# Turning q and k over two slots, x^T in halves, and the last four weight conversions moved behind the first batch

## The chip, the cores and the metric

The kernel runs on one core of a Trainium2 chip. The metric is device time in microseconds, the median of several executions.

## The reference

Attention with a threshold, for 8 batches of 8 heads, 576 rows and head size 64, then a two-layer MLP with exact GELU over the 4608 rows of 512:

```python
scores = scale * np.matmul(q, k.transpose(0, 1, 3, 2))
thresh = np.max(scores, axis=-1, keepdims=True) - tau
scores = np.where(scores >= thresh, scores, -1000000000.0)
attn = np.exp(scores - np.max(scores, axis=-1, keepdims=True))
attn = attn / (np.sum(attn, axis=-1, keepdims=True) + 1e-09)
attn_out = np.matmul(attn, v)
x = attn_out.transpose(0, 2, 1, 3).reshape(B * S, H * D)
h = x @ w_in
out = (0.5 * h * (1.0 + erf(h / sqrt(2)))) @ w_out
```

q, k, v are float32. The MLP's weights (512x2048 and 2048x512) arrive as 64-bit floats, so the kernel has to turn them into float32 itself.

## The kernel before

**Slots.** Two heads make a pair; a pair p has five chunks of query rows (four of 128 rows for each head, the fifth with the 64 left of both). One (pair, chunk) is a slot n, and the order of the work is a list written out by hand (lines 1103 to 1107): slots 0 to 7 take chunks 0 and 1 of the four pairs of batch 0, slots 8 to 19 their chunks 2 to 4, and from slot 20 (`BATCH`) on each pair goes through its five chunks in turn, pairs 4 to 31. All instructions of a slot are issued in the order of the loop body at line 1137, and each engine keeps to that order.

**What a slot does.** `scores` (L400) multiplies on TensorE into one or two PSUM tiles "sc", of which there are two buffers. `softmax_head` takes the row maximum on VectorE (L412), the threshold on GpSimd (L415) and the exponential on ScalarE (L417). `softmax_tail` masks and sums on VectorE (L433), and so frees the "sc" buffers for the next slot's scores. In the first batch p is transposed on TensorE one slot later (`turn_p_early`, L347, with copies by ScalarE at L354 and L362); from pair 4 on VectorE transposes it (`turn_p`, L532) and DMAs regroup it. `weigh_v` (L571) multiplies with v to x^T; the early `weigh_half` (L603) does it for one chunk of 128 rows. All TensorE outputs other than scores share four PSUM buffers "mm"; each is free again when its copy has been made.

**Turning q and k.** In the first batch `turn_qk_early` transposes q and k of the next pair on TensorE (L317, and L327 for the tails of 64 rows); ScalarE copies them out (L320 and L322, tails L330 and L331, and the two q tails at L334). It is called once in the first slot of the pair before (line 1150), that is in slots 0, 2 and 4 for pairs 1, 2 and 3. Raw q and k of pair 2 lie in two slots of `xall`.

**x^T of the first batch.** A list `due` names what is multiplied with v in the next slot. Pairs 2 and 3 (`HALVED`) have x^T of their first 256 rows made in two halves, in slots 6 to 9; pairs 0 and 1 have it made whole, in slots 3 and 5. `divide_early` (L490, L492, L498) follows with the second half or the whole.

**Weights.** 32 pieces of 128x512 are loaded as raw 64-bit values, pieces 0 to 15 of w_in and 16 to 31 of w_out; even ones go to a slot of `xall` (seven slots, some of which hold x), odd ones to a part of `turned_p`, apart from the last `LATER`, which go to `xall` too. A conversion has three parts: two activations on ScalarE (`convert_first`, L199 and L200), two operations on VectorE (`convert_second`, L207 and L208), and one add on GpSimd (`add_low_bits`, L219). The add is issued in the next slot's `softmax_head`: that of the newest piece ahead of the first L415, the others behind the second. `STEPS` says how many conversions a slot ends with. The intermediate `power` comes from the pool "g" of 10 buffers, which also holds the hidden activations of an MLP block.

**The MLP in between.** `fill` issues the products of MLP blocks of 256 rows between the attention's work: the hidden layer at L671, the output layer at L686, up to a goal for each slot. A product is issued only when the number of pieces whose add has been issued is large enough: j of the output layer needs 17 + j. The hidden layer of block 0 lies in slots 10 to 19. In slot 20 its held GELUs run (L644), and in slot 21 the output layer begins. The last part of the kernel (from line 1260) runs ten blocks with a fast scheme on sums of tiles (L859, L741).

Of the kernel before, what the change touches and what calls it, by code (L numbers as in the profile page):

```python
# [9 lines left out]
U32 = mybir.dt.uint32  # L10
U8 = mybir.dt.uint8
AF = mybir.ActivationFunctionType
# [6 lines left out]
def kernel(  # L19
# [28 lines left out]
    nc = tc.nc  # L48
    ctx.enter_context(tc.manual_schedule())

    B, H, S, D = q.shape
    d_model, d_ff = moe_w_in.shape
    P = 128
    Q = 32
    HP = H // 2
    NP = B * HP
    EARLY = HP
    NC = S // P
    MAIN = NC * P
    TAIL = S - MAIN  # L60
# [5 lines left out]
    TOK = 256  # L66
# [32 lines left out]
    x_free = list(range(XSLOTS))  # L99
    x_at = {}  # L100

    def x_slot(want=None):
        i = max(x_free) if want is None else want
        x_free.remove(i)
        return i
# [8 lines left out]
    def x_rows(i):  # L114
        return xall[:, i, :, :].rearrange("p c t -> p (c t)")
# [5 lines left out]
    ident = const.tile([P, P], FP32, name="ident")  # L121
# [3 lines left out]
    q_tail = [att.tile([P, P], FP32, name=f"q_tail{i}") for i in range(4)]  # L125
# [3 lines left out]
    pd = [turned_p[:, e, :, :, :].rearrange("p h b i -> p (h b i)") for e in range(2)]  # L129
# [8 lines left out]
    q_scale = const.tile([P, 1], FP32, name="q_scale")  # L138
# [7 lines left out]
    for _ in range(3):  # L146
# [3 lines left out]
    PIECE = 512  # L150
    pieces = [(w_in_sb[c][:, f:f + PIECE], moe_w_in[c * P:(c + 1) * P, f:f + PIECE])
              for f in range(0, d_ff, PIECE) for c in range(N_DM)]
    pieces += [(w_out_sb[j][:, f:f + PIECE], moe_w_out[j * P:(j + 1) * P, f:f + PIECE])
               for j in range(N_DF) for f in range(0, d_model, PIECE)]
    wide = moe_w_in.dtype != FP32
    LATER = 2
    raws = []
    loaded = [0]
    converted = [0]

    def load_piece(eng=nc.sync):
        k = loaded[0]
        if k == len(pieces):
            return
        staged = k % 2 and k < len(pieces) - LATER
        if wide and not staged and not x_free:
            return
        dst, src = pieces[k]
        loaded[0] += 1
        if not wide:  # L170
            nc.sync.dma_start(dst, src)
            converted[0] += 1
            load_piece()
            return
        slot = []
        if staged:

            half, at = divmod(k // 2 % 4, 2)
            raw = pd[half].bitcast(U32)[:, at * 2 * PIECE:(at + 1) * 2 * PIECE]
        else:  # L180
            slot = [x_slot()]
            raw = x_rows(slot[0]).bitcast(U32)
        eng.dma_start(raw, src.bitcast(U32))
        raws.append((dst, raw, slot))

    ahead = []

    def convert_first():

        dst, raw, slot = raws.pop(0)
        lo, hi = (raw.rearrange("p (f w) -> p f w", w=2)[:, :, i] for i in range(2))
        power = gp.tile([P, PIECE], U32, tag="g", name="power")
        nc.scalar.activation(power.bitcast(FP32), hi.bitcast(FP32), AF.Copy, bias=0.0, scale=2.0 ** -112)  # L199
        nc.scalar.activation(dst.bitcast(U32), lo, AF.Copy, bias=0.0, scale=2.0 ** -29)  # L200
        ahead.append((dst, hi, power, slot))
# [20 lines left out]
    def convert_ahead(steps):  # L222

        while raws and len(ahead) <= steps:
            convert_first()

    def convert(steps):

        while steps > 0 and (ahead or raws):
            convert_ahead(1)  # L230
            convert_second()
            steps -= 1

# [62 lines left out]
            for c in range(2):  # L296
                nc.tensor.matmul(idle[:, c * P:(c + 1) * P], lhsT=ident, rhs=ident, start=True, stop=True)

    def turn_qk_early(p):


        s = st[p]
        if 2 <= p < HP:
            qT = op.tile([P, MAIN], FP32, tag="o_sb", name="qT")
            kT = pd_tail[p - 2].rearrange("p b i -> p (b i)")
        else:
            qT = ld.tile([P, MAIN], FP32, tag="qT", name="qT")
            kT = ld.tile([P, TAIL + S], FP32, tag="kT", name="kT")
        s["qT"], s["kT"] = qT, kT
        qt = s["q_tail"] = q_tail[p % 4]  # L310
        copy = nc.scalar.copy if p else nc.vector.tensor_copy
        for name in "qk":
            t = s[name]
            tr = ps.tile([P, NC, P], FP32, tag="mm", name="tr")
            for c in range(NC):
                for e in range(2):
                    nc.tensor.matmul(tr[e * D:(e + 1) * D, c, :], lhsT=t[:, e, c, :], rhs=ident, start=True, stop=True)  # L317
            src = tr.rearrange("p c s -> p (c s)")
            if name == "q":
                nc.scalar.activation(qT, src, AF.Copy, bias=0.0, scale=q_scale)  # L320
            else:
                copy(kT[:, TAIL:S], src)  # L322
        tr = ps.tile([P, NC, P], FP32, tag="mm", name="tr")
        for j, name in enumerate("qk"):
            t = s.pop(name)
            for e in range(2):
                nc.tensor.matmul(tr[e * D:(e + 1) * D, j, 0:TAIL], lhsT=t[0:TAIL, e, NC, :],  # L327
                                 rhs=ident[0:TAIL, 0:TAIL], start=True, stop=True)
        x_free.extend(s.pop(name + "_slot") for name in "qk" if name + "_slot" in s)
        nc.scalar.copy(kT[:, S:S + TAIL], tr[:, 1, 0:TAIL])  # L330
        nc.scalar.copy(kT[D:P, 0:TAIL], tr[D:P, 1, 0:TAIL])  # L331
        for e in range(2):
            rows = slice(e * D, (e + 1) * D)
            nc.scalar.activation(  # L334
                qt[rows, e * TAIL:(e + 1) * TAIL], tr[rows, 0, 0:TAIL], AF.Copy, bias=0.0, scale=q_scale[rows])

    def turn_p_early(p, i):

# [140 lines left out]
    def divide_early(p, lo, hi):  # L479


        s = st[p]
        b, hp = divmod(p, HP)
        tr = ps.tile([P, 512], FP32, tag="mm", name="tr")
        for i in range(lo // P, -(-hi // P)):
            den = s.pop(("sum", i))
            to = tr[:, i * P - lo:min((i + 1) * P, hi) - lo]
            for e in range(2):
                one_of, cols = (den[:, e:e + 1], ident) if i < NC else (den, ident[:, e * TAIL:(e + 1) * TAIL])
                nc.tensor.matmul(to[e * D:(e + 1) * D, :], lhsT=one_of.to_broadcast([P, D]), rhs=cols, start=True, stop=True)  # L490
        by = dg.tile([P, S], FP32, tag="inv", name="inv")
        nc.scalar.copy(by[:, 0:hi - lo], tr[:, 0:hi - lo])  # L492
        for n, o, at, size in in_blocks(b, lo, hi):
            x, y = x_blk[n][:, hp, o:o + size], by[:, at - lo:at - lo + size]
            if size == TOK:
                x = x.rearrange("q (p c) -> q c p", c=2)
                y = y.rearrange("q (c p) -> q c p", c=2)
            nc.gpsimd.tensor_tensor(x, x, y, op=ALU.mult)  # L498
# [595 lines left out]
    for _ in range(4):  # L1094
        load_piece(nc.sync)
# [12 lines left out]
    BATCH = HP * SLOTS  # L1108
# [15 lines left out]

    PARTS = 1.3, 1.3, 0.2, 1.3, 0.9

    HALVED = (2, 3)
    DIVIDE_LATE = {14: 0, 16: 1, 19: 2, 22: 3}
    STEPS = [0, 1, 1, 1, 1, 1, 2, 1, 2, 2, 2, 2, 3, 2, 2, 3, 2, 2, 2]
    BUSY = {1: 2, 6: 2, 8: 2}  # L1130

    tokens = 0
# [1 line left out]
    due = []  # L1134
    leaving = []
    loads = iter(())
    for n in range(len(slots) + WEIGH + 1):
        p, i = slots[n] if n < len(slots) else divmod(n, SLOTS)
        early = p < EARLY
        last = slots[n - 1] if 0 < n <= len(slots) else None  # L1140
        if p < NP:
            scores(p, i)
            softmax_head(p, i)
            add_low_bits()
            if last and last[0] < EARLY and last[1] < 2:
                invert(*last)
            if last and last[0] < EARLY and last[1] == NC:
                divisors_early(last[0])
            if p < HP - 1 and i == 0:
                turn_qk_early(p + 1)  # L1150
        elif n == len(slots):
            early_end.close()
            weights_first()
# [5 lines left out]
        for args in due:  # L1159
            if len(args) == 2:  # L1160
                weigh_half(*args)
                if args[1]:
                    divide_early(args[0], 0, TOK)
                continue
            if n == BATCH:
                xT = weigh_v(*args, None)
                continue
            weigh_v(*args)
            if args[1] == 0:
                divide_early(*args)  # L1170
        due = []
        if long:
            convert_ahead(STEPS[n] if n < BATCH - 1 else LATER)
        if n in DIVIDE_LATE:
            divide_late(DIVIDE_LATE[n])
        if p > EARLY and i == WEIGH:
# [51 lines left out]
            scale_q(p + 1)  # L1228
        if p >= HP - 1 and i == 2 and p + 1 < NP:
            turn_qk(p + 1)  # L1230
        convert(STEPS[n] if n < BATCH - 1 else len(pieces))
        if not early:
            lag[0] = 2 if p < NP else 0
            if n != BATCH:
# [3 lines left out]
        if n in BUSY:  # L1238
            keep_busy(BUSY[n])
        if last and last[0] < EARLY:  # L1240
            if last[1] < 2 and last[0] in HALVED:
                due.append((last[0], last[1]))
            elif last[1] == 1:
                due.append((last[0], 0, TOK))
            if last[1] == NC and early:
                due.append((last[0], TOK, S))
            if n == BATCH - 1:
                due.append((p, TOK, S))
# [44 lines left out]
```

## Time and profile before

| | |
|---|---|
| median of three executions | 1331.73 us (1331.51 to 1331.79) |
| the profiled execution, its own time | 1331.37 us |
| its span, first to last instruction | 1329.2 us |
| TensorE busy | 1315.9 us |
| VectorE busy | 1040.7 us |
| ScalarE busy | 604.3 us |
| GpSimd busy | 635.2 us |
| granted TensorE clock | 0.999 |

Cut at the first L412 of each slot, the slots that the change touches took:

| slot | window, us | length | PE busy | DVE busy | ACT busy | POOL busy |
|---|---|---|---|---|---|---|
| 2 | 18.65 to 23.48 | 4.83 | 4.39 | 4.08 | 4.59 | 2.38 |
| 3 | 23.48 to 29.16 | 5.68 | 5.63 | 4.39 | 5.38 | 2.64 |
| 4 | 29.16 to 34.00 | 4.84 | 4.81 | 4.09 | 4.72 | 2.58 |
| 5 | 34.00 to 39.69 | 5.69 | 5.63 | 4.43 | 5.45 | 2.46 |
| 6 | 39.69 to 44.94 | 5.25 | 5.18 | 5.03 | 5.18 | 2.16 |
| 7 | 44.94 to 49.84 | 4.90 | 4.69 | 4.54 | 4.64 | 4.03 |
| 18 | 112.86 to 118.93 | 6.07 | 4.84 | 5.04 | 4.57 | 3.44 |
| 21 | 129.62 to 138.01 | 8.39 | 8.39 | 4.28 | 6.65 | 3.29 |
| 22 | 138.01 to 144.24 | 6.23 | 6.23 | 5.94 | 1.41 | 4.20 |
| 23 | 144.24 to 148.77 | 4.53 | 4.53 | 4.28 | 1.99 | 3.00 |

How to read it: PE is TensorE, DVE VectorE, ACT ScalarE, POOL GpSimd, SP the engine that issues most DMAs. A matmul's end is modelled, so a busy PE is not PE at its peak, and each float32 product is recorded as two matmuls. In a timeline line the first number is the start, the second the length; "x8" merges eight instructions; what stands in brackets at the end is the idle time before it and the instruction that ended it. The window of slot n starts with its L412, while its scores were made in the end of the window before.

### The profile page before, as it was taken

The page shows a single profiled execution, that of the slowest core. Times are in us where ns is not written, and L with a number is a line of the kernel's source. Part 1 is how long each engine was busy: PE and PEld are TensorE (multiplying, and loading weights), DVE is VectorE, ACT ScalarE, POOL GpSimd, SP SyncE. Part 2 cuts the span into 40 slices and gives each one's busy share as a digit, 9 for nine tenths or more (in the row PEclk, how much of TensorE's full clock was granted, in tenths as well). Part 3 has the DMA queues.
Part 4 walks back from the last instruction along what each step waited for, and adds up shares of the span by engine and source line. Part 5 has one row for each costly group of instructions (what it writes and reads, how often), then busy time and mean ns, then how long its engine had stood idle before and what let it go on. Part 6 is the DMA issues. An engine that isn't in the chain of part 4 may idle for free.

```text
span 1329.2 us, 19865 instructions
## 1 busy us (share of the span) xinstructions
PE 1315.9 (99%) x6306; PEld 891.0 (67%) x6306; DVE 1040.7 (78%) x2001; ACT 604.3 (45%) x1027; POOL 635.2 (48%) x1058
## 2 busy tenths in 40 slices
PE   9999999999999999999999999999999999999998
PEld 6766466476476466466466466468778787877877
DVE  6887787788888888888888888883857698386674
ACT  7987356367367358358458338232111203211120
POOL 3555445555655655655655641236264403645430
PEclk9999999999999999999999999999999999999999
DMA  8553666777877887787787775500000140000003
GB/s 260 166 179 88 141 150 160 169 162 159 191 170 156 192 186 157 193 198 162 184 207 159 176 174 108 106 9 0 1 0 1 40 105 15 0 1 0 1 0 79
DMA packets 213687, 153.14 MB, mean 115 GB/s; under 512 B 117264, under 2 KB 196992, under 8 KB 213584
## 3 DMA queue, kind: packets, MB, share of 16 engines
q1 hardware_dynamic: 195440, 125.31, 40.7%
q0 software_dynamic: 17712, 26.26, 7.6%
q8 instruction: 52, 0.85, 0.3%
q14 instruction: 51, 0.42, 0.1%
q10 hardware_dynamic: 432, 0.30, 0.1%
HBM read 56.62 MB, written 12.58 MB: 52 GB/s over the span
## 4 chain that ended last, share of the span: by engine, by line
PE 93%; DVE 3%; ACT 2%; issue 1%; DMA 0%; POOL 0%; DVEq 0%; ACTq 0%; POOLq 0%
PE bank L859 34%; PE o_ps L686 17%; PE hT L671 16%; PE sc L400 13%; PE xT L571 11%; DVE nmx L412 1%; ACT p L417 1%; DVE power L208 1%; DVE p L433 1%; DVE power L207 1%; PE tr L347 1%; DMA q<-in_q_dram 0%; ACT pT L354 0%; PE tr L317 0%; PE idle L147 0%
## 5 line engine op out<-in xcount | busy, mean ns | idle before, releaser
L417 ACT ACTIVATE p<-sc,nmx 128x576 f32<-128x576 f32 x288 | 201.9, 737 | 280.9 <-DVE nmx L412 280.7
L433 DVE SCALAR_TENSOR_TENSOR p<-sc,thr,p 128x576 f32<-128x576 f32 x288 | 225.3, 816 | 72.6 <-ACT p L417 66.1
L415 POOL TENSOR_SCALAR thr<-nmx,tau_eff 128x1 f32<-128x1 f32 x288 | 83.9, 293 | 340.2 <-DVE nmx L412 338.1
L671 PE MATMUL hT<-xall,w_in 128*128 128x256 f32 x1024 | 241.9, 386 | 0.0
L412 DVE TENSOR_REDUCE nmx<-sc 128x1 f32<-128x576 f32 x288 | 205.4, 750 | 44.9 <-PE sc L400 43.7
L686 PE MATMUL o_ps<-w_out,g 128*128 128x512 f32 x512 | 236.8, 603 | 0.2 <-ACT g L644 0.2
L671 PEld LDWEIGHTS hT<-xall,w_in 128*128 128x128 f32 x1024 | 189.7, 190 | 51.1 <-issue 24.5
L741 DVE TENSOR_TENSOR o<-o,bank 128x256 f32<-128x256 f32 (+1 forms) x242 | 100.2, 418 | 94.3 <-PE bank L859 89.3
L741 DVE TENSOR_TENSOR c<-c,bank 128x320 f32<-128x320 f32 x304 | 147.1, 488 | 34.2 <-PE bank L859 21.0
L686 PEld LDWEIGHTS o_ps<-w_out,g 128*128 128x128 f32 x512 | 93.2, 190 | 109.5 <-issue 106.7
L400 PE MATMUL sc<-kT,qT 64*128 64x288 f32 x960 | 160.5, 429 | 1.9 <-DVE p L433 1.2
L571 PE MATMUL xT<-pT,v 128*64 128x320 f32 (+1 forms) x1240 | 159.4, 410 | 0.2
L532 DVE STREAM_TRANSPOSE turned_p<-p 128x1152 f32<-128x1152 f32 x112 | 154.4, 1378 | 3.9
L400 PEld LDWEIGHTS sc<-kT,qT 64*128 64x128 f32 x960 | 91.9, 186 | 75.8 <-issue 60.8
L571 PEld LDWEIGHTS xT<-pT,v 128*64 128x64 f32 x1240 | 86.4, 137 | 70.8 <-issue 11.1
L859 PE MATMUL bank<-w_out,c 128*128 128x256 f32 (+1 forms) x484 | 120.5, 380 | 0.8 <-DVE o L741 0.8
L260 POOL DMA_DIRECT2D v<-in_v_dram x208 | 110.8, 536 | 3.7 <-issue 1.6
L859 PEld LDWEIGHTS bank<-w_out,c 128*128 128x128 f32 x484 | 90.4, 190 | 18.8 <-DVE o L741 3.2
L926 ACT ACTIVATE c<-c 128x320 f32<-128x320 f32 (+1 forms) x80 | 46.9, 624 | 115.0 <-DVE c L741 114.9
L859 PE MATMUL bank<-t_out,g 128*128 128x256 f32 (+1 forms) x324 | 82.5, 377 | 0.4 <-DVE o L741 0.4
L859 PE MATMUL bank<-t_out,c 128*128 128x256 f32 x320 | 82.8, 381 | 0.0
L741 POOL TENSOR_TENSOR c<-c,g 128x320 f32<-128x320 f32 (+1 forms) x40 | 50.5, 1271 | 67.5 <-DVE c L741 67.5
(185 smaller groups left out, 1751.2 us busy)
## 6 DMA issues: line engine op xcount, KB each, us to landing
pT<-turned_p SPq DMA_DIRECT2D x448, 160.0 KB, 3.6
pT<-pd_tail SPq DMA_DIRECT2D x112, 80.0 KB, 3.0
q<-in_q_dram POOLq DMA_DIRECT2D x104, 72.0 KB, 3.6
k<-in_k_dram POOLq DMA_DIRECT2D x104, 72.0 KB, 3.3
inv<-turned SPq DMA_DIRECT2D x54, 128.0 KB, 4.1
v<-in_v_dram POOLq DMA_DIRECT2D x156, 40.0 KB, 3.1
out_dram<-o SPq DMA_DIRECT2D x40, 128.0 KB, 2.4
xall<-in_moe_w_out_dram SPq DMA_DIRECT2D x9, 512.0 KB, 4.7
```

Source lines behind the costliest of these rows:

```text
L260: eng.dma_start(t[r:P:4, e, 0:n, :], rows[:, r * KR:r * KR + n, :])
L400: nc.tensor.matmul(sc[e][:, h, 0:HALF], lhsT=lhsT, rhs=s["kT"][rows, at:at + HALF], start=True, stop=True)
L412: nc.vector.tensor_reduce(nmx[:, e:e + 1], sc, axis=AXIS.XY, op=ALU.max, negate=True)
L415: nc.gpsimd.tensor_scalar(thr[:, e:e + 1], nmx[:, e:e + 1], -1.0, tau_eff, op0=ALU.mult, op1=ALU.subtract)
L417: nc.scalar.activation(w[:, e * S:(e + 1) * S].rearrange("p (h s) -> p h s", h=2), sc, AF.Exp, bias=nmx[:, e:e + 1], scale=1.0)
L433: nc.vector.scalar_tensor_tensor(row, sc[e][:, :, 0:HALF], thr[:, e:e + 1], row, op0=ALU.is_ge, op1=ALU.mult, accum_out=den[e])
L532: nc.vector.transpose(turned_p[:, :, i // 2, 0:NB, i % 2 * Q:(i % 2 + 1) * Q], w.rearrange("p (e b i) -> p e b i", e=2, i=Q))
L571: nc.tensor.matmul(to, lhsT=s["v"][:, e, c, :], rhs=rhs, start=(c == 0), stop=(c == KR - 1))
L671: nc.tensor.matmul(hT[:, j % 2, :], lhsT=w_in_sb[c][:, j * P:(j + 1) * P], rhs=x_blk[n][:, c, :], start=(c == 0), stop=(c == N_DM - 1))
L686: nc.tensor.matmul(o[:, 0:d_model], lhsT=g[j][:, m * P:(m + 1) * P], rhs=w_out_sb[j], start=(j == 0), stop=(j == N_DF - 1))
L741: eng.tensor_tensor(out, a, b, op=ALU.add)
L859: nc.tensor.matmul(to, lhsT=l, rhs=r, start=start and k == 0, stop=k == len(pairs) - 1, skip_group_check=not start)
```

## The change

- `turn_qk_early` takes the names it turns. Pairs 2 and 3 are turned in two slots: q in slot 2 or 4, k in slot 3 or 5. Pair 1 is still turned in slot 0. Each part has a PSUM tile for its tails.
- The q tails of both heads leave PSUM in one copy of 128x128; two products with a block of zeros fill the quadrants between them.
- All pairs of the first batch have x^T of their first 256 rows made in two halves.
- `STEPS` has one conversion less in slots 2, 4, 6 and 18, and two each in slots 21 and 22, where a conversion is begun only when it is finished (`ahead_of=0`). The pieces concerned are 28 to 31, of w_out.
- The last four pieces are loaded into slots of `xall`, and a load that finds no slot is kept and asked for again later.

```diff
-    LATER = 2
+    LATER = 4
...
+    wanted = [0]
...
     def load_piece(eng=nc.sync):
-        k = loaded[0]
-        if k == len(pieces):
-            return
-        staged = k % 2 and k < len(pieces) - LATER
-        if wide and not staged and not x_free:
-            return
...
+        wanted[0] += 1
+        while wanted[0] > 0 and loaded[0] < len(pieces):
+            k = loaded[0]
+            staged = k % 2 and k < len(pieces) - LATER
+            if wide and not staged and not x_free:
+                return
...
+            wanted[0] -= 1
...
-    def convert(steps):
+    def convert(steps, ahead_of=1):
 
         while steps > 0 and (ahead or raws):
-            convert_ahead(1)
+            convert_ahead(ahead_of)
             convert_second()
             steps -= 1
...
-    def turn_qk_early(p):
+    def turn_qk_early(p, names="qk"):
...
-        for name in "qk":
+        for name in names:
...
-        for j, name in enumerate("qk"):
+        for j, name in enumerate(names):
             t = s.pop(name)
             for e in range(2):
-                nc.tensor.matmul(tr[e * D:(e + 1) * D, j, 0:TAIL], lhsT=t[0:TAIL, e, NC, :],
+                at = e * TAIL if name == "q" else 0
+                nc.tensor.matmul(tr[e * D:(e + 1) * D, j, at:at + TAIL], lhsT=t[0:TAIL, e, NC, :],
                                  rhs=ident[0:TAIL, 0:TAIL], start=True, stop=True)
...
-        nc.scalar.copy(kT[:, S:S + TAIL], tr[:, 1, 0:TAIL])
-        nc.scalar.copy(kT[D:P, 0:TAIL], tr[D:P, 1, 0:TAIL])
+        if "k" in names:
+            nc.scalar.copy(kT[:, S:S + TAIL], tr[:, j, 0:TAIL])
+            nc.scalar.copy(kT[D:P, 0:TAIL], tr[D:P, j, 0:TAIL])
+        if "q" not in names:
+            return
+        none = q_tail[HP - 1][0:TAIL, D:2 * D]
         for e in range(2):
-            rows = slice(e * D, (e + 1) * D)
-            nc.scalar.activation(
-                qt[rows, e * TAIL:(e + 1) * TAIL], tr[rows, 0, 0:TAIL], AF.Copy, bias=0.0, scale=q_scale[rows])
+            nc.tensor.matmul(tr[e * D:(e + 1) * D, 0, (1 - e) * TAIL:(2 - e) * TAIL], lhsT=ident[0:TAIL, 0:D],
+                             rhs=none, start=True, stop=True)
+        nc.scalar.activation(qt, tr[:, 0, :], AF.Copy, bias=0.0, scale=q_scale)
...
-    HALVED = (2, 3)
...
-    STEPS = [0, 1, 1, 1, 1, 1, 2, 1, 2, 2, 2, 2, 3, 2, 2, 3, 2, 2, 2]
+    STEPS = [0, 1, 0, 1, 0, 1, 1, 1, 2, 2, 2, 2, 3, 2, 2, 3, 2, 2, 1, 0, 0, 2, 2]
...
-            if p < HP - 1 and i == 0:
-                turn_qk_early(p + 1)
+            if p == 0 and i == 0:
+                turn_qk_early(1)
+            elif p < HP - 1 and i < 2 and n > 1:
+                turn_qk_early(p + 1, "qk"[i])
...
-            convert_ahead(STEPS[n] if n < BATCH - 1 else LATER)
+            convert_ahead(STEPS[n])
...
-        convert(STEPS[n] if n < BATCH - 1 else len(pieces))
+        convert(STEPS[n] if n < len(STEPS) else 0, 1 if n < BATCH else 0)
...
-            if last[1] < 2 and last[0] in HALVED:
-                due.append((last[0], last[1]))
-            elif last[1] == 1:
-                due.append((last[0], 0, TOK))
+            if last[1] < 2:
+                due.append(last)
```

More of the change, by code (lines that the diff above doesn't have):

```diff
@@ L155 @@
     wide = moe_w_in.dtype != FP32
-    LATER = 2
+    LATER = 4
     raws = []
     loaded = [0]
+    wanted = [0]
     converted = [0]
     def load_piece(eng=nc.sync):
-        k = loaded[0]
-        if k == len(pieces):
-            return
-        staged = k % 2 and k < len(pieces) - LATER
-        if wide and not staged and not x_free:
-            return
[L168 to L184, printed above, removed]
+        wanted[0] += 1
[4 more added lines that the diff above has]
+                return
+            dst, src = pieces[k]
+            loaded[0] += 1
+            if not wide:
+                nc.sync.dma_start(dst, src)
+                converted[0] += 1
+                continue
+            wanted[0] -= 1
+            slot = []
+            if staged:
+                half, at = divmod(k // 2 % 4, 2)
+                raw = pd[half].bitcast(U32)[:, at * 2 * PIECE:(at + 1) * 2 * PIECE]
+            else:
+                slot = [x_slot()]
+                raw = x_rows(slot[0]).bitcast(U32)
+            eng.dma_start(raw, src.bitcast(U32))
+            raws.append((dst, raw, slot))
     ahead = []
@@ L297, in keep_busy @@
                 nc.tensor.matmul(idle[:, c * P:(c + 1) * P], lhsT=ident, rhs=ident, start=True, stop=True)
-    def turn_qk_early(p):
+    def turn_qk_early(p, names="qk"):
         s = st[p]
-        if 2 <= p < HP:
+        if names == "k":
+            qT, kT = s["qT"], s["kT"]
+        elif 2 <= p < HP:
             qT = op.tile([P, MAIN], FP32, tag="o_sb", name="qT")
@@ L323, in turn_qk_early @@
         tr = ps.tile([P, NC, P], FP32, tag="mm", name="tr")
-        for j, name in enumerate("qk"):
+        for j, name in enumerate(names):
             t = s.pop(name)
             for e in range(2):
-                nc.tensor.matmul(tr[e * D:(e + 1) * D, j, 0:TAIL], lhsT=t[0:TAIL, e, NC, :],
+                at = e * TAIL if name == "q" else 0
+                nc.tensor.matmul(tr[e * D:(e + 1) * D, j, at:at + TAIL], lhsT=t[0:TAIL, e, NC, :],
                                  rhs=ident[0:TAIL, 0:TAIL], start=True, stop=True)
-        x_free.extend(s.pop(name + "_slot") for name in "qk" if name + "_slot" in s)
-        nc.scalar.copy(kT[:, S:S + TAIL], tr[:, 1, 0:TAIL])
-        nc.scalar.copy(kT[D:P, 0:TAIL], tr[D:P, 1, 0:TAIL])
+        x_free.extend(s.pop(name + "_slot") for name in names if name + "_slot" in s)
+        if "k" in names:
[4 more added lines that the diff above has]
+        none = q_tail[HP - 1][0:TAIL, D:2 * D]
         for e in range(2):
-            rows = slice(e * D, (e + 1) * D)
-            nc.scalar.activation(
-                qt[rows, e * TAIL:(e + 1) * TAIL], tr[rows, 0, 0:TAIL], AF.Copy, bias=0.0, scale=q_scale[rows])
+            nc.tensor.matmul(tr[e * D:(e + 1) * D, 0, (1 - e) * TAIL:(2 - e) * TAIL], lhsT=ident[0:TAIL, 0:D],
+                             rhs=none, start=True, stop=True)
+        nc.scalar.activation(qt, tr[:, 0, :], AF.Copy, bias=0.0, scale=q_scale)
     def turn_p_early(p, i):
@@ L1168 @@
             weigh_v(*args)
-            if args[1] == 0:
-                divide_early(*args)
         due = []
         if long:
-            convert_ahead(STEPS[n] if n < BATCH - 1 else LATER)
+            convert_ahead(STEPS[n])
         if n in DIVIDE_LATE:
```

## The prediction

> **What bounds the kernel now.** I read the page's busy shares and chain first, then the chain of waits for 0 to 180 us, then a table of windows cut at the first maximum (L412) of each slot, then the timeline of the slots that the change touches.
>
> ```profile
> PE   9999999999999999999999999999999999999998
> PE 93%; DVE 3%; ACT 2%; issue 1%; DMA 0%; POOL 0%; DVEq 0%; ACTq 0%; POOLq 0%
> ```
>
> The first line is TensorE's busy share over time, the second the engines' shares of the chain that ended last. From about 129 us on TensorE has no hole: listed by what PE waits for, all waits after 165 us come to 1.3 us. So a microsecond that PE loses after 129 us is added to the end, and one that the slots before 129 us save comes off it. Before 129 us the chain of waits alternates:
>
> ```profile
> 22.24 0.31 ACT q_tail L334
> 22.89 0.59 ACT pT L354
> 23.53 2.54 PE xT L571 x19
> ...
> 48.32 0.89 DVE power L207
> 49.23 0.69 DVE power L208
> 49.93 1.34 DVE nmx L412 x2
> ...
> 129.37 7.11 PE o_ps L686 x16
> 136.47 1.55 PE sc L400 x8
> 138.02 2.77 PE o_ps L686 x6
> 140.80 1.72 PE sc L400 x8
> 142.52 4.49 PE o_ps L686 x10
> ```
>
> Columns: start, length, engine and line. In slots 2 to 5 (18.65 to 39.69 us) PE and ACT pace each other; from slot 6 on VectorE paces (softmax, then conversion, then the next maximum); from slot 21 it is PE alone. The slots where the four conversions go are these, on VectorE:
>
> ```profile
> 135.11 0.82 DVE L433 SCALAR_TENSOR_TENSOR p<-sc,thr,p 128x576 f32<-128x576 f32 x1 [4.08 <-ACT p L417]
> ...
> 136.71 1.38 DVE L532 STREAM_TRANSPOSE turned_p<-p 128x1152 f32<-128x1152 f32 x1
> 138.01 1.39 DVE L412 TENSOR_REDUCE nmx<-sc 128x1 f32<-128x576 f32 x2
> ...
> 143.76 0.45 DVE L388 STREAM_TRANSPOSE q_tail<-q 64x64 f32<-64x64 f32 x2
> 144.24 1.42 DVE L412 TENSOR_REDUCE nmx<-sc 128x1 f32<-128x576 f32 x2
> ```
>
> VectorE idles 4.08 us in slot 21, but **ahead** of L433; behind it, to 148.77, it is busy almost without a break. And PE's scores of slot 23 start at 140.72 against an L433 of slot 22 that ends at 141.2: no slack.
>
> **What the skill says.** The Trainium skill, "PSUM — Partial Sum Buffer", section "Engine vs sequencer instructions": the queues of ScalarE, VectorE and GpSimdE are strict FIFO, and matmuls start in program order. The trace agrees: L207 follows L433 in each early slot. So a conversion written after slot 21's L433 can't use the 4.08 us ahead of it. "TensorE: Matmul & The Clock Gate", section "HAM oscillation — how this bites in real kernels": no PE gap above some 3.4 us, or the clock falls. The page of before has full clock in every slice, so nothing here shows it; I use it only for the range. "ScalarE: Activation LUTs", section "What ACT_TABLE_LOAD costs": an ACTIVATE has a fixed part of 186 ns or more. The trace has 0.63 us for the two 64x64 copies of L334 and 0.21 for one 64x64 copy (L331), so merging two saves about one.
>
> **Part by part.**
>
> *q tails in one copy* (four pairs). Off ACT: 0.63 us; on: one 128x128 copy with a pointer scale, bounded by 0.28 (L362, same size) and 0.36; I take 0.30. It saves 0.3 us of ACT a pair. On PE two zero products of 64x64 are added, about 0.1 us by L327 (8 records in 0.45). Pairs 0 and 1: L330 and L331 are ahead of it and feed the scores, so nothing gained or lost there.
>
> *Turning in two slots and halves of x^T* (pairs 2 and 3 turned in slots 2/3 and 4/5; x^T of pairs 0 and 1 there). PE occupancy from starts to starts: scores 1.17, q or k 0.95 each, tails 0.38, L571 with N=256 2.67, its half (L603) 1.24, L490 0.54, nine L347 1.13. Slot 2: before 1.17 + 1.90 + 0.38 + 1.13 = 4.6, after 1.17 + 0.95 + 0.3 + 1.24 + 1.13 = 4.8. Slot 3: before 1.17 + 2.67 + 0.54 + 1.13 = 5.5, after 1.17 + 0.95 + 0.2 + 1.24 + 0.54 + 1.13 = 5.25. PE's sum stays at 10.1 us for two slots which now take 4.83 + 5.68 = 10.5. ACT's work of slot 2 falls: without k (L322, L330, L331: 0.93 by starts), 0.3 of the q tail and, by STEPS, without a conversion (L199 and L200, 1.15), with a 0.2 copy added. So pT (L354) is done 1 us earlier, and exp of slot 3, now at 25.31 behind that conversion, starts at 24.27. It does not help slot 2 itself: the scores of slot 3 wait for L433 at 22.03 as before. Laying out slots 3, 4 and 5 with these rows (four "mm" banks, each freed by its ACT copy) they come to 5.39, 4.60 and 5.38 against 5.68, 4.84 and 5.69: **0.3 + 0.24 + 0.3 us** off.
>
> *One conversion less in slots 2, 4, 6 and 18.* On VectorE one is L207 + L208, 1.06 us from start to start. In slots 2 and 4 it lies beside the 1.2 us of scores (L412 of slot 3 waits 0.37 for PE): nothing beyond the above. Slot 6 has two and is VectorE-paced; with one, L412 waits for the scores: **0.5 us**, and 0.15 in slot 7, where L433 no longer waits for POOL's second add. In slot 18 the ACT half of a conversion stays (one is begun there to be ahead), and L412 waited 0.57 us for PE anyway: 0. Slots 8 to 17 do the same count on other pieces. Sum of the early part: **-1.5 us**; bounds -0.5 (an ACT copy is late for a bank in each pair) and -2.6 (slots 2 to 7 all at the 4.76 of slot 6's loop, 31.2 - 6 x 4.76).
>
> *Loads.* `wanted` only keeps refused requests; I followed the slots of xall through: pieces 28 to 31 are asked for in slots 15 to 17, at least four slots, over 20 us, ahead of use, while a piece lands in 4.7 us. SP's queue gets no more issues. 0.
>
> *Conversions in slots 21 and 22* (times of before; subtract 1.5). Queued behind them on VectorE is the next L412, and behind that exp, L433 and PE's next scores. Slot 21: two conversions, 2.12 us, between L532 (ends 138.09) and L412: L412 at 140.13. The add of the newest piece now stands on POOL ahead of L415: where that is so now, L433 starts 1.8 us after L412 (slots 8 to 10), else 1.6: +0.2. L433 of slot 22 ends at 143.5, not 141.2; PE's scores of slot 23 wait for it, **2.3 us**. Slot 22: L532, turn_qk (1.75) and two more conversions: L412 of slot 23 at 144.24 + 2.12 + 0.2 + 2.12 = 148.7. ACT's halves (1.15 each) fit in its idle time there, and their `power` buffers are free (8 of 10 hold g). Now the new wait: fill(23) has the products j = 11 to 15 of L686, and j = 14 needs w_out piece 30, whose add stands on POOL behind that of piece 31 and both L415; in slot 9 such a second add ends 3.27 us after L412 starts (55.21 to 58.48). So at 151.97 PE may go on: two products of 0.9 each, done at 153.75, where L686 ends at 147.01 now: **+6.7 us**. The scores of slot 25, which now take 1.99 instead of 1.24 because L433 of slot 24 is late, lose that wait: -0.7. Sum **+6.0 us**. If the adds were in time, the scores of slot 24 would still wait for L433 of slot 23, 4.6 us later than now: +3.9 is the lower end. From above: a PE gap of 4.7 us before j = 14 might lower the clock for a few us, +2.
>
> Sum: 1331.37 (the profiled execution, span 1329.2) - 1.5 + 6.0 = 1335.9; the median 1331.73 is 0.36 higher, so **1336.2 us**.
>
> **Rivals.**
> *Only VectorE's delay counts and the early part is at its floor:* +3.9 - 2.6 = +1.3, 1333.0. For: slots 6 and 7 run at 4.8 without turning. Against: slots 3 and 5 have 5.25 us of PE work. 0.17.
> *The PE gap also costs clock, or the add comes later behind POOL's k loads (2.7 us):* +6.0 + 2 + 0.5 (less early gain) - 1.5 = +7, 1338.7. 0.18.
> *Faster:* the early part is paced by ACT alone, so all that leaves it there counts: three conversions of 1.15 and two q tails of 0.3, 4.1 us off; and PE's queue covers the late conversions. That gives 1327.6. It beats 0.2% only if the late stall stays under 1.4 us, a quarter of what I find; for it speaks ACT's 4.59 us busy of 4.83 in slot 2, against it that PE is at 5.63 of 5.68 in slot 3. 0.08.
> That the change does not do what it says: the conversions could be held back by missing loads; the bookkeeping above excludes it.
>
> **How the numbers follow.** Forecast 0.57, rivals 0.17, 0.18 and 0.08. About 0.2% (2.7 us) is what a measurement here can tell from no change. The forecast's case and the costlier one are slower, the cheap one lies within: slower 0.75, same 0.17, faster 0.08. Range 1333.0 (the cheap case's time) to 1339.2 (late +8, early -0.5): about 2 in 10 lie outside, mostly below.
>
> **What would show it.** Right: slots 2 to 7 end 1 to 2 us earlier; L207 and L208 stand behind L532 in slots 21 and 22; L412 of slots 22 and 23 come 2.1 and 4.4 us later against slot 20's start; PE's waits list L400 <- L433 and L686 <- POOL L219 with 2 and 4 us. Wrong: PE without such waits after 129 us, or the start of L686 in slot 21 earlier by over 3 us.

## The result, and the profile after

Over six executions of each, the changed kernel takes 1339.14 us (1338.12 to 1341.75), the kernel before 1331.64 (1330.61 to 1331.79). The ratio is 1.0060, with a 95% interval of 1.0047 to 1.0073 (the quotient of the two medians, 1.0056, lies inside it): **slower, by 6.3 to 9.7 us**. The forecast was +4.5 and the top of its range +7.5: the difference of the medians, 7.5, lies at that top, and the interval mostly above it. The profiled execution of the changed kernel took 1340.47 us, 9.1 more than that of before.

In the changed kernel L412 is L420, L433 is L441, L400 is L408, L686 is L694, L671 is L679, L532 is L540, L207 and L208 are L208 and L209, and L219 is L220. Its page has these two rows, to be held against those of before in the prediction:

```profile
PE   8999899999999999999999999999999999999998
PE 91%; DVE 3%; DMA 2%; ACT 2%; issue 1%; SPq 1%; POOL 1%; DVEq 0%; POOLq 0%; ACTq 0%
```

TensorE has two slices more that are not full, the first and the fifth (134 to 167 us); the chain now leads through DMAs and SP's queue as well. What TensorE waited for from 126 to 165 us (columns: in total, times, longest):

```profile
PE o_ps L694 <- POOL w_out L220: 4.4, 1, 4.4
PE sc L408 <- DVE p L441: 2.1, 1, 2.1
```

and up to 130 us, one more line that the kernel before does not have:

```profile
PE tr L341 <- ACT kT L336: 1.9, 2, 1.4
```

L341 is the product with the block of zeros, L336 ScalarE's second copy of the k tails. The wait of 1.4 us is in slot 0, where pair 1 is turned; the scores of slot 1 stand right behind it (first two lines), while in the kernel before (third line) they waited 0.32 us for a mask:

```profile
13.09 0.33 PE L341 MATMUL tr<-q_tail,ident 64*64 64x64 f32 x4 [1.39 <-ACT kT L336]
13.35 1.24 PE L408 MATMUL sc<-kT,qT 64*128 64x288 f32 x8
...
12.13 1.94 PE L400 MATMUL sc<-kT,qT 64*128 64x288 f32 x8 [0.32 <-DVE p L433]
```

On VectorE, slots 21 to 23 look like this in the timeline:

```profile
136.22 1.38 DVE L540 STREAM_TRANSPOSE turned_p<-p 128x1152 f32<-128x1152 f32 x1
137.52 0.38 DVE L208 TENSOR_SCALAR power<-power 128x512 uint32<-128x512 uint32 x1
...
139.00 0.69 DVE L209 SCALAR_TENSOR_TENSOR power<-xall,power 128x512 uint32<-128x512 uint32 x1
139.61 1.41 DVE L420 TENSOR_REDUCE nmx<-sc 128x1 f32<-128x576 f32 x2
...
147.59 0.69 DVE L209 SCALAR_TENSOR_TENSOR power<-xall,power 128x512 uint32<-128x512 uint32 x1
148.20 1.42 DVE L420 TENSOR_REDUCE nmx<-sc 128x1 f32<-128x576 f32 x2
```

The conversions stand behind the transpose, and the maxima of slots 22 and 23 start at 139.61 and 148.20 instead of 138.01 and 144.24. TensorE at the same place:

```profile
142.40 1.94 PE L408 MATMUL sc<-kT,qT 64*128 64x288 f32 x8 [2.10 <-DVE p L441]
144.28 2.84 PE L694 MATMUL o_ps<-w_out,g 128*128 128x512 f32 x6
151.52 3.01 PE L694 MATMUL o_ps<-w_out,g 128*128 128x512 f32 x4 [4.41 <-POOL w_out L220]
154.33 1.84 PE L408 MATMUL sc<-kT,q_tail 128*128 128x288 f32 x4
```

Both waits are there, and something else: four records of L694 take 3.01 us, where six take 2.84 just before, and the scores of slot 24 take 1.84 instead of the 1.21 of before. The table of windows has the granted clock (third number from the end) of slot 23:

```profile
148.20:156.21 8.01, 4.69 (x9) 2.53 (x10) 4.35 (x9) 1.99 (x3) 5.45 (x9) 0.79 0.24 60
152.40:155.70 3.30, 3.30 (x6) 1.66 (x5) 0.59 (x1) 0.58 (x1) 1.77 (x4) 0.50 0.45 109
```

The second line, a narrower window, shows what the 0.79 is made of: the clock stood at one half for some 3.4 us and at full before and behind. The first line agrees: 0.21 of 8.01 us lost is 1.7 us, or half the clock for 3.4 us.

For everything that follows I took from each kernel's timeline the start of the first maximum of each slot, counted from that of slot 0, and subtracted the same of the kernel before. That shows where a kernel gains and loses, free of the differences of up to 0.8 us, against the kernel before, in when slot 0 starts. Each row is one profiled execution; where two kernels do the same up to a slot, their rows agree within 0.03 us:

| us later than before, at slot | 1 | 8 | 21 | 25 | 100 | 131 |
|---|---|---|---|---|---|---|
| changed kernel | +1.01 | -0.75 | -0.44 | +7.52 | +7.49 | +9.20 |
| e1, zero products first | 0.00 | -1.77 | -1.49 | +4.77 | +4.76 | +6.68 |
| e2, turns only | +1.01 | +0.24 | +0.22 | +0.22 | +0.19 | +0.20 |
| e3, conversions only | -0.01 | -1.00 | -0.61 | +5.65 | +5.98 | +6.13 |
| e4, q tails only | +1.01 | +2.67 | +2.66 | +2.66 | +2.67 | +3.55 |
| e5, busy in the gap | +1.00 | -0.75 | -0.45 | +5.82 | +5.99 | +9.33 |
| e6, two products later | +1.00 | -0.76 | -0.44 | +5.26 | +5.99 | +5.99 |
| e7, two in slot 21 | +1.00 | -0.76 | -0.77 | +1.54 | +1.50 | +4.97 |
| e8, one in slot 19 | -0.01 | -1.76 | +1.00 | +1.01 | +1.03 | +1.18 |
| e9, one begun in 18 | -0.01 | -1.77 | -1.79 | -1.79 | -1.79 | -0.35 |
| e10, shift only | 0.00 | 0.00 | -0.05 | +4.12 | +4.12 | +5.02 |
| e11, two tail copies | -0.01 | -1.67 | -1.71 | -1.72 | -1.70 | -1.60 |

The changed kernel loses 1.0 in slot 0, gains 1.76 in slots 1 to 7, gives 0.3 back by slot 21, loses 7.96 in slots 21 to 24, and in this execution 1.7 more after slot 100.

One loss lies ahead of slot 0, and so outside the table. The zero products of pair 0 wait 0.53 us for the same copy for which the first scores waited 0.50 us in the kernel before, and then delay those scores. From the start of the transposition of pair 0's k tails to the start of the first scores it takes 1.07 us in the changed kernel and 0.78 in the kernel before; in all six kernels with the zero products behind those copies (the changed one, e2, e4, e5, e6, e7) it is 1.07 to 1.08, in the other seven 0.70 to 0.78. So 0.3 us more are lost there.

### The profile page after: what moved, and what is told of

Its sections match the earlier page's. It is cut to its first block, busy times and chain, and to the rows that moved or that the text cites. A ratio compares the mean times of both kernels' runs of the same rounds, so it can differ in the third digit from the quotient of the medians.

```text
span 1338.3 us, 19973 instructions
## 1 busy us (share of the span) xinstructions
PE 1316.8 (98%) x6362; PEld 891.2 (67%) x6362; DVE 1039.2 (78%) x2001; ACT 603.4 (45%) x1025; POOL 636.0 (48%) x1058
## 4 chain that ended last, share of the span: by engine, by line
PE 91%; DVE 3%; DMA 2%; ACT 2%; issue 1%; SPq 1%; POOL 1%; DVEq 0%; POOLq 0%; ACTq 0%
PE bank L867 34%; PE o_ps L694 16%; PE hT L679 16%; PE sc L408 13%; PE xT L579 10%; DVE nmx L420 1%; DMA inv<-turned 1%; PE tr L355 1%; DVE p L441 1%; DMA turned<-turned 1%; ACT p L425 1%; PE tr L320 1%; DVE power L209 0%; DVE power L208 0%; PE xT L611 0%
## 5 line engine op out<-in xcount | busy, mean ns | idle before, releaser
L441 DVE SCALAR_TENSOR_TENSOR p<-sc,thr,p 128x576 f32<-128x576 f32 x288 | 225.2, 815 | 72.3 <-ACT p L425 63.4
L420 DVE TENSOR_REDUCE nmx<-sc 128x1 f32<-128x576 f32 x288 | 205.4, 750 | 55.8 <-PE sc L408 54.7
L694 PE MATMUL o_ps<-w_out,g 128*128 128x512 f32 x512 | 238.0, 605 | 4.6 <-POOL w_out L220 4.4
L679 PE MATMUL hT<-xall,w_in 128*128 128x256 f32 x1024 | 241.9, 385 | 0.0
L679 PEld LDWEIGHTS hT<-xall,w_in 128*128 128x128 f32 x1024 | 189.3, 190 | 51.4 <-issue 24.5
L694 PEld LDWEIGHTS o_ps<-w_out,g 128*128 128x128 f32 x512 | 93.1, 190 | 114.7 <-issue 106.9
L408 PE MATMUL sc<-kT,qT 64*128 64x288 f32 x960 | 159.3, 428 | 4.8 <-DVE p L441 4.8
L540 DVE STREAM_TRANSPOSE turned_p<-p 128x1152 f32<-128x1152 f32 x112 | 154.4, 1378 | 3.9
L579 PE MATMUL xT<-pT,v 128*64 128x320 f32 (+1 forms) x1200 | 154.2, 410 | 0.0
L408 PEld LDWEIGHTS sc<-kT,qT 64*128 64x128 f32 x960 | 91.2, 186 | 78.3 <-issue 63.5
L579 PEld LDWEIGHTS xT<-pT,v 128*64 128x64 f32 x1200 | 83.7, 137 | 68.2 <-issue 11.1
```

Source lines behind the costliest of these rows:

```text
L408: nc.tensor.matmul(sc[e][:, h, 0:HALF], lhsT=lhsT, rhs=s["kT"][rows, at:at + HALF], start=True, stop=True)
L420: nc.vector.tensor_reduce(nmx[:, e:e + 1], sc, axis=AXIS.XY, op=ALU.max, negate=True)
L441: nc.vector.scalar_tensor_tensor(row, sc[e][:, :, 0:HALF], thr[:, e:e + 1], row, op0=ALU.is_ge, op1=ALU.mult, accum_out=den[e])
L540: nc.vector.transpose(turned_p[:, :, i // 2, 0:NB, i % 2 * Q:(i % 2 + 1) * Q], w.rearrange("p (e b i) -> p e b i", e=2, i=Q))
L579: nc.tensor.matmul(to, lhsT=s["v"][:, e, c, :], rhs=rhs, start=(c == 0), stop=(c == KR - 1))
L679: nc.tensor.matmul(hT[:, j % 2, :], lhsT=w_in_sb[c][:, j * P:(j + 1) * P], rhs=x_blk[n][:, c, :], start=(c == 0), stop=(c == N_DM - 1))
```

## The experiments

My theory after the result: four terms, namely a wait at the zero products, which I had not seen (+1.0); the turning spread over two slots and fewer early conversions (-1.8); VectorE's and GpSimd's lateness in slots 21 to 23 (about +6.3); and a fall of TensorE's clock behind its gap (+1.7). The rivals: the rearrangement is itself a loss; each moved conversion costs the same; the long durations in slot 23 are not the clock's. Each time below is a median, and each ratio is to the kernel before, run beside it. The line numbers in an experiment's timeline are those of its own kernel.

**e1, zero products first.** The wait has a plain form in the program: the zero products write the PSUM tile that holds the k tails, and were issued behind ScalarE's copies of those.

```diff
+        if "q" in names:
+            none = q_tail[HP - 1][0:TAIL, D:2 * D]
+            for e in range(2):
+                nc.tensor.matmul(tr[e * D:(e + 1) * D, 0, (1 - e) * TAIL:(2 - e) * TAIL], ...)
         if "k" in names:
             nc.scalar.copy(kT[:, S:S + TAIL], tr[:, j, 0:TAIL])
...
-        none = q_tail[HP - 1][0:TAIL, D:2 * D]
-        for e in range(2):
-            nc.tensor.matmul(...)
         nc.scalar.activation(qt, tr[:, 0, :], AF.Copy, bias=0.0, scale=q_scale)
```

> The changed kernel, with the two zero products of each q tail put ahead of ScalarE's two copies of the k tails. Theory: in slot 0 TensorE stood 1.4 us at the zero products, which waited for those copies, and the scores of slot 1 behind them; the wait goes, and with it 1.0 us: 1338.1, and the first maximum of slot 1 at 13.7 instead of 14.6 us. Rival (slot 1 is later because of the wider copy and the extra products themselves): 1339.1, the maximum stays at 14.6.

It takes 1337.95 us against 1331.94, ratio 1.0042 (1.0030 to 1.0055). In slot 0 neither the zero products (L337) nor the scores of slot 1 wait any more:

```profile
11.68 0.28 PE L337 MATMUL tr<-q_tail,ident 64*64 64x64 f32 x4
12.05 1.94 PE L409 MATMUL sc<-kT,qT 64*128 64x288 f32 x8
```

Slot 1 starts at 13.59 us, and from there to slot 21 the kernel is 1.0 to 1.05 ahead of the changed one. The theory holds for the wait; by the medians alone it would not be shown, as the two intervals overlap. That the median came out at the 1338.1 expected is partly luck: by slot 25 the kernel is 2.75 ahead, as the clock's fall cost it nothing (see e3), and after slot 100 its profiled execution lost 1.9.

**e2, turns only.** The changed kernel with the counts and the loads of before (`LATER = 2`, the old `STEPS` and `convert`).

> The turning in two slots, the halves and the single copy of the q tails, with all conversions where they were before. Theory: +1.0 in slot 1, and in slots 2 to 5 a gain of some 0.5, as ScalarE keeps its conversions there: +0.5, 1332.1. Rival (spreading q and k is itself what gained 1.8 us between slots 2 and 8): -0.8, 1330.8. Rival (the rearrangement is itself a loss, by its additional PSUM tiles): +1.5 or more.

It takes 1332.40 us, ratio 1.0006 (0.9998 to 1.0014), and in the table it is 0.2 later than before from slot 8 on. So the turning and halving gain 0.8 by slot 6 (+1.01 to +0.25) without any conversion moved, and the wait at the zero products takes it back. The rearrangement is not a loss in itself, and it is not the whole gain of 1.8 either: both rivals fall. Which of the two, turning or halving, gains the 0.8 is not separated by any run.

**e3, conversions only.** The kernel before with `LATER`, `load_piece`, `STEPS` and `convert` of the changed one.

> The kernel before, with only the conversions moved (counts per slot, the four last pieces, the kept requests). Theory: all of the late cost, +8.0, and a gain of some 0.7 in slots 2 to 8: +7.3, 1338.9, with TensorE waiting 2.1 us for the mask of slot 22 and 4.4 us for GpSimd's add in slot 23. Rival (the late cost needs the new turning as well): less than half of it, below 1335.5.

It takes 1337.81 us, ratio 1.0050 (1.0037 to 1.0063). It gains 1.0 by slot 8, which with the 0.8 of e2 makes up the changed kernel's 1.76, and loses 6.26 in slots 21 to 24: the late cost is the conversions' own, and does not need the new turning. The 8.0 expected included the fallen clock, which cost nothing here. TensorE's second wait was only 2.76 us instead of 4.41, since the clock fell behind the first gap: the scores and the six records of L687 (L694 of the changed kernel) ahead of the second wait took 2.76 and 3.67 us instead of 1.94 and 2.84, together 1.65 more. In the timeline of e3:

```profile
145.46 3.67 PE L687 MATMUL o_ps<-w_out,g 128*128 128x512 f32 x6
151.88 1.98 PE L687 MATMUL o_ps<-w_out,g 128*128 128x512 f32 x4 [2.76 <-POOL w_out L220]
153.71 1.13 PE L401 MATMUL sc<-kT,q_tail 128*128 128x288 f32 x4
```

A slow TensorE ahead of a wait that ends on GpSimd cost nothing here; in the changed kernel it was slow behind it.

**e4, q tails only.** The kernel before with the single copy and its zero products.

> The kernel before, with only the q tails of both heads in one copy. Theory: the zero products wait for the copies of the k tails in all three later pairs; +1.0 in slot 1, and up to 0.3 more in slots 2 and 4, where TensorE has less to wait behind: +1.2, 1332.8. Rival (ScalarE's 0.3 us a pair is what counts): -0.6, 1331.0.

It takes 1335.40 us, ratio 1.0030 (1.0019 to 1.0041). The +1.0 came as expected; the "up to 0.3 more" was far off, it is 1.66, in slots 2 and 4, where pairs 2 and 3 are turned. In e4's list of waits (L335 the zero products, L332 the second copy of the k tails, which for pairs 2 and 3 goes to `pd_tail`):

```profile
PE tr L335 <- ACT pd_tail L332: 3.2, 2, 1.8
PE tr L335 <- ACT kT L332: 1.9, 2, 1.4
```

Where q and k are turned together, as in the kernel before, the zero products wait for every pair; the changed kernel escapes this for pairs 2 and 3 because their k tails have a tile of their own and are turned a slot later.

**e5, busy in the gap.** Products that nobody needs fill the gap.

```diff
+                if (n, m, j) == (0, 0, N_DF - 2):
+                    keep_busy(7)
```

> The changed kernel, with 28 products of ident by ident (about 4.0 us) for TensorE ahead of the product with weight piece 30, where it stood 4.4 us. Nothing else moves. Theory: the clock fell to 0.72 after the gap and the next four products and scores took 1.85 us more for it; with TensorE busy it stays: -1.8, 1337.3. Rival (the longer durations are not the clock's): no change, 1339.1, or later by what the added products overrun.

The 0.72 of the expectation is the mean clock from 150 to 156 us. Here the clock stayed at full in slots 21 to 25, and the products behind the gap are back at their length:

```profile
146.63 3.29 PE L298 MATMUL idle<-ident 128*128 128x128 f32 x28
151.20 1.98 PE L696 MATMUL o_ps<-w_out,g 128*128 128x512 f32 x4 [1.29 <-POOL w_out L220]
153.03 1.13 PE L408 MATMUL sc<-kT,q_tail 128*128 128x288 f32 x4
```

By slot 25 it is 1.70 ahead of the changed kernel (+5.82 against +7.52). The time does not show it: 1340.47, ratio 1.0062 (1.0049 to 1.0075). The profiled execution lost 3.3 us after slot 100, 3.1 of it in slots 129 and 130; where the others lost it was not traced. So the clock's part is shown for that place, in one profiled execution of each kernel, and the expectation of 1337.3 was missed.

**e6, two products later.** The products of pieces 30 and 31 wait until slot 24 (a further condition in `fill`).

> The changed kernel, with the products of pieces 30 and 31 held back until slot 24, so that slot 23 does not wait for GpSimd's adds. Theory: VectorE's delay is right behind: the scores of slot 24 then wait for the mask of slot 23, which ends 0.7 us ahead of that add: about -0.7, 1338.4, with a TensorE gap of nearly 4 us that is now named after the mask. Rival (the add on GpSimd is the cause of its 4.4 us): -4.4, 1334.7.

It takes 1338.60 us, ratio 1.0048 (1.0035 to 1.0060). GpSimd's add is out of the way, and the mask of slot 23 is found behind it at once:

```profile
146.07 4.86 PE L694 MATMUL o_ps<-w_out,g 128*128 128x512 f32 x6
151.73 1.21 PE L408 MATMUL sc<-kT,q_tail 128*128 128x288 f32 x4 [0.80 <-DVE p L441]
```

The clock had fallen behind the first gap, so that TensorE filled most of that time with slow products, at no cost. Slot 24 starts 1.6 us earlier than in e5, which has no clock loss there either (+4.20 against +5.79 in the measure of the table), but now the products held back run in that slot: by slot 25 the lead is 0.56, and by slot 100 nothing is left (+5.99 both). So the rival falls: the 4.4 us named after GpSimd do not come back when its add is passed by, since VectorE's mask (151.58 us, its first half) ends only 0.64 us ahead of that add (152.22). What an earlier add would bring is another question, which no run asks: TensorE could then make those products ahead of the mask.

**e7, two in slot 21.** `STEPS` has one conversion again in slots 2 and 4, and none in slot 22.

> The changed kernel, with two of the four moved conversions put back to slots 2 and 4 (where VectorE waits for TensorE's scores anyway), so that slot 21 keeps two and slot 22 none. Theory: the wait of 2.1 us for the mask of slot 22 stays, the 4.4 us and the fallen clock go: +2.3 - 0.7 (scores of slot 25) - 0.5 to 0 early: +1.5, 1333.1. Rival (each moved conversion costs the same): half of 8.0, less the early gain: +3.5, 1335.1.

By slot 25 it is at +1.54, and by slot 8 at the same -0.76 as the changed kernel: conversions in slots 2 and 4 cost nothing. Slots 21 to 24 lose 2.31 with two conversions and 6.27 with four (without the clock), so the rival of equal prices falls. The sum met the +1.5 of the theory by luck in its parts: the 0.7 at the scores of slot 25 was not gained (they take 1.99 us as in the kernel before), and the early gain was larger. The time missed the 1333.1: the median is 1336.44, ratio 1.0031 (1.0019 to 1.0042), and the six executions range from 1332.62 to 1337.65. The profiled one lost 3.5 us in slots 129 and 130:

```profile
683.84 1.69 POOL L627 TENSOR_TENSOR xall<-xall,inv 128x128 f32<-128x128 f32 x3 [1.94 <-DMA inv<-turned]
...
688.01 0.82 DVE L441 SCALAR_TENSOR_TENSOR p<-sc,thr,p 128x576 f32<-128x576 f32 x1 [2.66 <-POOL thr L423]
688.98 1.21 PE L408 MATMUL sc<-kT,qT 64*128 64x288 f32 x6 [1.47 <-DVE p L441]
690.12 5.41 PE L679 MATMUL hT<-xall,w_in 128*128 128x256 f32 x16
```

The DMA of the divisors lands 2 us late for GpSimd; GpSimd divides x, issues the loads of v and only then computes the threshold; VectorE and TensorE follow; and behind a gap of 1.5 us the clock stands at 0.50 for some 3.4 us and L679 takes 5.41 us instead of 3.72.

**e8, one in slot 19.** Zero products first, one conversion in each of slots 1 to 7, two in slot 18 and the last one in slot 19.

> The new turning with the zero products put first, one conversion in each of slots 1 to 7, and the one so left over in slot 19, where VectorE waits 3.2 us for the scores and ScalarE has done its part a slot ahead. Theory: slots 2 to 8 keep most of their 1.8 us, slot 0 loses nothing, slots 9 to 19 give back some 0.3, and nothing is late after slot 20: -1.2, 1330.4. Rival (conversions in slots 2 and 4 are what counted): -0.5 or less, 1331.1 or more.

It takes 1332.14 us, ratio 1.0005 (0.9997 to 1.0013): a miss, and my edit's fault. With two for slot 18, ScalarE began two conversions ahead of the copies of pT:

```profile
116.14 0.33 PE L356 MATMUL tr<-ident,p 128*128 128x128 f32 x1 [2.02 <-ACT pT L363]
116.30 1.14 PE L409 MATMUL sc<-pd_tail,q_tail 128*128 128x288 f32 x4
117.28 4.44 PE L680 MATMUL hT<-xall,w_in 128*128 128x256 f32 x12
```

TensorE stood 2.02 us instead of 0.9, and L680 then took 4.44 us instead of 2.75: 1.1 and 1.7 us, the 2.8 that this kernel loses between slots 18 and 20.

**e9, one begun in slot 18.**

```diff
-            convert_ahead(STEPS[n])
+            convert_ahead(min(STEPS[n], 1) if n == BATCH - 2 else STEPS[n])
```

> As the kernel with one conversion in slot 19, but only one conversion is begun on ScalarE ahead of the copies of pT in slot 18 (there two were, TensorE stood 2.0 us for pT, and the products after it took 4.44 instead of 2.75 us). Theory: both losses go, the 1.75 us gained by slot 8 stay to the end: 1330.2 against 1331.9. Rival (something else in slots 18 and 19 is late): 1331.5 or more.

In the table it stands at about -1.8 from slot 8 to slot 100, as expected, and L680 is at 2.75 us. The time is less clear: 1331.16 against 1332.13, ratio 0.9993 (0.9985 to 1.0000), where 1330.2 against 1331.9 was expected. Its executions range from 1328.9 to 1334.5, and the profiled one gave 1.4 back after slot 100.

**e10, shift only.** The kernel before with `BUSY[21] = 10`.

> The kernel before, with 40 products of ident by ident for TensorE at the end of slot 21, so that all later work starts some 5 us later, with TensorE busy in between and nothing else changed. It asks whether the further 1 to 3 us that some runs lose near slot 130, where GpSimd waits for the DMA of the divisors, come with any late shift. Theory (they do not depend on the change): the shift alone, 5 to 6 us, and in some executions 1 to 3 us more: 1337 to 1340. Rival (they need what the change does): the shift alone in all executions, within 0.5 us of what slot 24 shows.

It takes 1336.58 us against 1332.13, ratio 1.0027 (1.0018 to 1.0037), its nine executions within 2.1 us. The added products shift by 4.12 us instead of 5 to 6, so the time is below the range expected. By slot 131 the profiled execution is at +5.02, but the 0.9 came in slots 107 and 127, not in 129 and 130. The highest of the nine is 1.0 above the median of before plus the shift. So neither expectation is met, and a mere shift of this size was not followed by 3 us in any of the nine.

**e11, two tail copies.** e9 without the single copy and the zero products.

> As the one begun in slot 18, but the q tails leave PSUM in two copies as in the kernel before, without zero products. Theory: the single copy saves 0.3 us of ScalarE a pair, which lies beside TensorE's work, and costs 0.1 us of TensorE: within 0.2 of the other, 1330.2. Rival (the single copy pays): 0.5 or more later.

It is at -1.72 at slot 25, so within 0.1 of e9: the single copy gains nothing worth having. It takes **1330.26** us against 1332.13, ratio 0.9982 (0.9973 to 0.9990): the only version whose interval lies wholly below 1, if by little. That its median is 0.9 below that of e9 fits what e9 lost after slot 100 in its profiled execution, and is not explained by the tails.

## Why the prediction was off

*Direction and place: right.* VectorE's strict order kept the conversions behind L540, and the maxima of slots 22 and 23 came 2.1 and 4.45 us later against slot 20, as forecast (2.1 and 4.4). TensorE waited 2.10 and 4.41 us where the prediction has 2.3 and 4.7, and the second wait bears GpSimd's name. Without the clock the late loss is 6.26 to 6.27 us (e1, e3, e5) against 6.0.

*The first step that failed* reads: "Pairs 0 and 1: L330 and L331 are ahead of it and feed the scores, so nothing gained or lost there." The new products were priced by their length (0.1 us), and what they wait for was left out. For pair 1 the copies stand in ScalarE's queue behind the exponentials of slot 0, the zero products wait for them, and behind those stand the scores of slot 1: +1.01 us. For pair 0 the scores had waited for the same copies already, and the products behind them add 0.3 us. e1 takes both losses away by order alone. (The copy of 128x128 itself took 0.37 us, above its bound of 0.36.)

*The second step that failed* is the clock: "a PE gap of 4.7 us before j = 14 might lower the clock for a few us, +2." This stood in the range and in a rival of chance 0.18, and the forecast put it at nothing, although its own working had this gap, and it is longer than the 3.4 us that the prediction quotes. The clock fell, and cost 1.70 us (changed kernel against e5), the larger of the two. Whether a fall costs depends on where it lands: in e1, e3 and e6 it came behind the first gap, in the shadow of the wait that follows.

*The early gain:* in sum right, in parts not. By slot 8 it is 1.76 against 1.5: the turning and halving 0.76 (0.84 forecast), slot 6 0.47 (0.5), slot 7 0.53 (0.15). Then 0.36 us are lost between slots 10 and 11, where the prediction had "Slots 8 to 17 do the same count on other pieces", by each kernel that has five conversions before slot 8 and by none that has seven or eight. In all of the former GpSimd's add at the head of slot 10 starts 0.58 us behind the slot's first maximum instead of 0.23, and the threshold behind it is late by the same; why the add starts late is not shown. That the gain is 1.45 at slot 21, so near to 1.5, is luck: two misses cancel.

*Sum at slot 25:* 1.0 - 1.76 + 0.3 + 6.27 + 1.7 = +7.5, which is 3.0 above the forecast: 1.0 from the wait, 1.7 from the clock, 0.3 from the late loss. That it is also the difference of the medians is partly chance, since the 0.3 us ahead of slot 0 and what is lost after slot 100 are not in it.

*After slot 100* the profiled execution lost 1.7 more. Six of the profiled executions (the changed kernel, e1, e4, e5, e7, e9) lost 0.9 to 3.5 us in slots 129 and 130, and in each GpSimd had stood 1.0 to 2.1 us ahead of its division (the trace names the DMA of the divisors in four of the six), in the others at most 0.3. In e5 and e7 the clock fell behind the gap that followed, which makes 1.7 us of their 3.1 and 3.5. Why it stands there in some executions and not in others stays open. The change may not be needed for it: among the 32 executions of the kernel before that ran beside e9 to e11, three took 1334.9 to 1335.4 us, 3 above their median, though none of these was traced.

## What to carry to other kernels

An added instruction is not only its own duration: ask what it waits for and what stands behind it in its queue; two small products into a PSUM tile that another engine was still reading, estimated at 0.1 us, cost 1.3 here. A conversion was free where its engine already waited for another (slots 2, 4 and 19). Where the next step of a tight loop stood behind it, it cost about its length on VectorE (two in slot 21: 2.3 us for 2.1 of work), and some 1.7 times that where a second wait hung on it (two more in slot 22: 4.0). When a wait is named after one engine, remove it and see which one is right behind.

## What the runs showed of the hardware that I had not expected

TensorE's granted clock fell behind gaps of 2.0 to 2.1 us (e1, e3, e6, e8) and even of 1.1 and 1.5 us (near slot 130 in e5 and e7), not only behind the 4.4 of the changed kernel. Each time it stood at 0.50, for some 3.4 us, in e6 for twice that. So the work after it took 1.7 us longer in e1 (in sum 6.44 instead of 4.78 for the next scores and L695), e3, e5, e7 and e8, and 3.1 in e6. It does not follow every such gap: in the changed kernel, e5 and e7 the same 2.1 us between slots 21 and 22 left the clock at full, and so did the second gap of e1 and e3, 2.76 us. What decides is not shown. The Trainium skill, "TensorE: Matmul & The Clock Gate", section "HAM oscillation — how this bites in real kernels", speaks of gaps above some 3.4 us; here shorter ones came before a fall in six of these kernels.
